# DeltaNet with a routed mixture of experts on one core: ScalarE's spread and table load moved, two products added in the prologue, the constants loaded in three pieces

## The chip, the core and the metric

The kernel runs on one core of one Trainium2 chip. Its metric is the device time of one execution in microseconds (us); three executions were timed, and their median counts. The engines are named TensorE (PE; PEld is its weight load), VectorE (DVE), ScalarE (ACT), GpSimd (POOL) and SyncE (SP, which issues most DMAs).

## The reference, cut to what matters

Per batch and head (4 x 8 of them, 768 steps, 48 columns) a state matrix is read and updated by the delta rule; the outputs of all heads of a token are one row x of 384 values, and each of the 3072 rows goes through the one expert that two softmaxes choose.

```python
k_n = k / (np.linalg.norm(k, axis=-1, keepdims=True) + 1e-06)
for t in range(S):
    y[:, :, t] = einsum('bhd,bhde->bhe', q[:, :, t], state)
    v_old = einsum('bhde,bhd->bhe', state, k_n[:, :, t])
    state = state + beta[t] * outer(k_n[:, :, t], v[:, :, t] - v_old)
x = y.transpose(0, 2, 1, 3).reshape(B * S, H * D)
# g = argmax(x @ w_group); e = argmax(x @ w_expert[g]); weights from two softmaxes
out[n] = g_w[n] * e_w[n] * (relu(x[n] @ w1[g, e]) @ w2[g, e])
```

## The kernel before

The recurrence is cut into 24 chunks of 32 steps (`NCH`, `C`). All four batches stand in the 128 partitions, 32 steps each, and the eight heads lie beside each other. Chunks form groups of four (`RG`). For a group the scores of keys with keys are collected in `gt`, and `inverse(g)` (from L351) turns them over into `m`, scales them, runs a long row of small VectorE products and sums (L428, L434) that solve the triangular system, and at last transposes the result into `mt` (L491). For groups 0 and 1 the norms take a root on ScalarE (L390), later ones do it on GpSimd.

The prologue makes the scores of chunks 0 to 9 in four PSUM homes (`early_gram`, `early_pairs`, L265 to L289) while VectorE inverts group 0. Key and query tiles come by `load_kq`, and a small ScalarE write ahead of each load (`begin`, L881 to L886) sets the time of its issue. `idle(home, n)` (L912) is a product into a PSUM tile that nobody reads: of the identity with the first n columns of the constants from the identity on. It stands twice at the end of the prologue, behind the scores of chunks 8 and 9.

Then the loop `for u in range(NCH + 1)` (L996) goes through the periods; period u advances chunk u (`advance`, L528):
- `begin_a` writes norms times v into PSUM (VectorE, L520, one period ahead); TensorE adds keys times state to it (`a_ps`, L536), ScalarE copies it out (`f`, L542), and TensorE starts `o_ps` (L548);
- `w_ps` (L556) is the inverse times f, read from `mtb`; ScalarE copies it (`w`, L559);
- `s_ps` (L566) adds to the state in PSUM, which ScalarE copies to `s_bd` (L574, two halves; from chunk 19 on one half by ScalarE, L576, and one by VectorE, L578). The next chunk's `a_ps` reads `s_bd`;
- `o_ps` is ended with the masked scores (L585 or L590), copied to `x` (L594), stored, transposed (`t_ps`, L612, `xt`, L618) and multiplied by the router (`l_ps`, L508, `lg`, L625) one period later;
- `gram(u + 10)` makes the scores ten chunks ahead (`g_ps`, L306) until period 13.

`spread(u)` (L336) writes `mtb`, the inverse of a chunk spread to two heads' halves by a factor of 0 or 1 per partition: two ScalarE copies of 128x256, one for each half (VectorE for chunk 0 alone). For the next chunk the front half stands behind `xt`, ahead of `s_bd`, and the back half behind `lg`, in all but the last periods. At the head of a group (u + 1 divisible by 4) both read the `mt` that VectorE has just written.

The order of instructions on each engine is the order in which the program is written, and each engine takes its instructions in that order. The VectorE steps of `inverse` and of the router (`route`) are laid between the steps of a period by `work(n)`, which hands out a budget in fixed portions; this order does not depend on times.

The constants are one array of 853 columns, cut by `cols` into two loads (`load_con`, L203): the first 100 columns at the very start, the other 753 (identity, `before`, `ones`, `desc`, `ids`, `quarter`, `places`, `tie`, `slots`, `expert`) behind the scores of chunk 6 in the prologue. ScalarE loads its function table for square roots at the start and the one for exponentials in period 0, by a dummy activation (L1040).

After the recurrence 16 experts follow (L1225, L1244), two matrix products each, with the gathering and scattering of rows on GpSimd.

Of the kernel before, what the change touches and what calls it, by code (L numbers as in the profile page):

```python
# [26 lines left out]
def constants(n_tokens, seq, n_experts, n_group, n_batch):  # L27

    import numpy as np

    p = np.arange(128)
    i, k = np.meshgrid(np.arange(C), np.arange(C), indexing="ij")
    u = np.arange(n_tokens // 128)

    ids = np.stack([(p[:, None] // C) * seq + p[:, None] % C + u * C - n_tokens,
                    u * 128 + p[:, None] + 1], axis=2)
    out = {
        "upper": np.concatenate([np.where(np.arange(2)[None, :, None] == b % 2, (i < k)[:, None], 0)
                                 .reshape(C, 2 * C) for b in range(n_batch)], axis=0),
        "causal": np.tile(i < k, (n_batch, 1)),  # L40
        "tiny": np.full((128, 1), 1e-36),
        "eps": np.full((128, 1), 1e-6),
        "parity": np.stack([p // C % 2 == b2 for b2 in range(2)], axis=1),
        "ident": (p[:, None] == p[None, :]),
        "before": (p[:, None] < p[None, :]),
        "ones": np.ones((128, 128)),
        "desc": np.tile(np.arange(n_group, 0, -1), (128, RG)),
        "ids": ids.reshape(128, -1),
        "quarter": p[:, None] // 32,

        "places": np.tile(np.arange(2 * TILE), (128, 1)),


        "tie": np.tile(n_experts - 1 - np.arange(n_experts) + (1 << 20) * (np.arange(n_experts) < FIXED), (128, 1)),
        "slots": np.tile(SLOTS, (128, 1)),
        "expert": np.tile(np.arange(n_experts), (128, 1)),
    }
    at, n = {}, 0
    for name, a in out.items():
        at[name] = (n, n + a.shape[1])  # L60
        n += a.shape[1]
    return np.concatenate([a.astype(np.float32) for a in out.values()], axis=1), at
# [3 lines left out]
def deltanet_then_moe(  # L66
# [110 lines left out]
    with ExitStack() as first:  # L177
# [20 lines left out]
        def load_kv(u):  # L198
            nc.sync.dma_start(out=kv_[u % NV], in_=kv_d[u])

        cols = [0, const_at["ident"][0], const_d.shape[1]]

        def load_con(i):  # L203
            part = slice(cols[i], cols[i + 1])
            nc.sync.dma_start(out=con[:, part], in_=const_d[:, part])
# [16 lines left out]
        def of_kv(u):  # L222
            return (kv_[u % NV], [lambda: load_kv(u)])

        def of_block(u):
# [4 lines left out]
            3: [of_kq(RG + 2)],  # L230
            RG: [of_kq(RG + 3), of_kq(0, 1)],
            RG + 1: [of_kq(u, 1) for u in range(1, RG)],
            RG + 2: [of_kv(0), (con[:, cols[1]:], [lambda: load_con(1)])],
            RG + 3: [of_kv(1), of_kq(2 * RG)],
            2 * RG + 1: [of_kq(2 * RG + 1), of_block(LEAD)],
            2 * RG + 3: [of_kq(2 * RG + 2), of_kv(2)],
# [18 lines left out]
        def early_gram(u, home, parts=(0, 1)):  # L255

            kqt = kqt_[u % NB]
            of = slice(parts[0], parts[-1] + 1)
            g_out = home.rearrange("p f (j x) -> p f j x", j=NP)[:, :, :, 0:2 * C].rearrange(
                "p f j (a t) -> p f j a t", a=2)  # L260
            for j in range(NP):
                for b in range(B):
                    for hh in range(2):
                        rows = slice(hh * 64, hh * 64 + D)
                        nc.tensor.matmul(g_out[quads[b], hh, j, of],  # L265
                                         lhsT=kqt[rows, 0, j, quads[b]],
                                         rhs=kqt[rows, of, j, quads[b]], start=True, stop=True,
                                         skip_group_check=True)
            for a in parts:
                nc.scalar.activation(scores(u, a), g_out[:, :, :, a], ACT.Copy)  # L270
# [606 lines left out]
        with tc.manual_schedule(engines={mybir.EngineType.PE, mybir.EngineType.DVE,  # L877
# [33 lines left out]
            nc.gpsimd.tensor_copy(what[:, :, 0:2], cut["ids"].rearrange("p (u c) -> p u c", c=2))  # L911
            def idle(home, n):  # L912

                nc.tensor.matmul(home[:, 0:n], lhsT=ident, rhs=con[:, cols[1]:cols[1] + n], start=True,
                                 stop=True, skip_group_check=True)

            for u in range(2 * RG, LEAD):
                early_gram(u, homes[u % len(homes)])
                begin(after_gram[u])
            idle(homes[2][:, 1], 512)  # L920
# [12 lines left out]
            second = inverse(1)  # L933
            next(second)
            next(second)
            mask(0)
            while leading in behind:
                push(leading)
# [57 lines left out]
            for u in range(NCH + 1):  # L996
# [25 lines left out]
                if u + 1 < NCH:  # L1022
                    mask(u + 1)
                known = u + 1 < NCH and (u + 1) // RG in mts
                if u == NCH - 1:
                    allow(PE_STEP)
                    allow(ACT_STEP)
# [7 lines left out]
                elif u < NCH - 3:  # L1035
                    next(step)
                    next(turned)
                    if u == 0:
                        begin(after_w)
                        nc.scalar.activation(rooted, cut["tiny"], ACT.Exp)  # L1040
                    if known:
                        spread(u + 1, [0])
                    allow(SORT)
                    next(step)
                    if u < NCH - NV:
                        load_kv(u + NV)
                    more_weights(u)
                    work(9)
                    next(step)
# [1 line left out]
                    allow(PE_STEP)  # L1051
                    allow(ACT_STEP)
                    if known:
                        spread(u + 1, [1])
                    for v in ahead_of[u]:
                        gram(v)
                    if ahead_of.get(u + 2):
# [401 lines left out]
```

## Time and profile before

| | us |
|---|---|
| median of 3 runs | 497.13 |
| lowest and highest | 489.25 and 498.51 |
| the profiled execution's own time | 495.36 |
| its span, from the first to the last instruction | 493.6 |
| mean granted TensorE clock in the span | 0.971 |
| busy: TensorE, VectorE, ScalarE, GpSimd | 455.2, 239.0, 191.6, 193.1 |

The profiled execution's time is 1.76 us over its span. A view by stretch gives busy times, a view of waits sums the idle time of an engine before an instruction under what ended it, and a timeline lists instructions in order of time. The busy time of TensorE is modelled and says less than its waits. [...]

### The profile page before, as it was taken

The numbers are of one execution on the slowest core, as the hardware profiler recorded it, in microseconds if no ns is written. First come the engines' busy times: TensorE is split into PE (matmuls) and PEld (weight loads), VectorE is DVE, ScalarE is ACT, GpSimd is POOL, SyncE is SP. The second block draws the span as 40 slices with busy tenths as digits, with TensorE's granted clock in tenths as the row PEclk, the third lists the DMA queues.
The fourth block names the chain that finished last, engine by engine and source line by source line (L and its number), as shares of the span: only waits on it lengthen the run. The fifth ranks groups of instructions, "written<-read, shape, count | busy, mean of one in ns | idle before, by whom it ended". The sixth has DMA issues, their size and how long they took to land.

```text
span 493.6 us, 17165 instructions
## 1 busy us (share of the span) xinstructions
PE 455.2 (92%) x7218; PEld 431.2 (87%) x7218; DVE 239.0 (48%) x834; ACT 191.6 (39%) x421; POOL 193.1 (39%) x322
## 2 busy tenths in 40 slices
PE   3669989999998998989999999999999999999992
PEld 3448878898987987879999999999999999999992
DVE  5999999999999855665211201220211111012210
ACT  3478688877865566551112112111211111111110
POOL 5000303716346213112456356545615653465313
PEclk9999999999996589999999999999999999999998
DMA  5987766776532335125978878957958987788751
GB/s 160 273 208 226 212 176 217 213 201 197 145 126 75 119 112 185 37 64 127 339 241 284 274 208 263 314 166 243 312 173 265 327 280 232 244 303 300 220 199 48
DMA packets 58579, 102.53 MB, mean 208 GB/s; under 512 B 19454, under 2 KB 41913, under 8 KB 58499
## 3 DMA queue, kind: packets, MB, share of 16 engines
q1 hardware_dynamic: 52579, 91.40, 59.4%
q0 software_dynamic: 5920, 10.00, 6.6%
q8 instruction: 58, 0.95, 0.9%
q14 instruction: 22, 0.18, 0.1%
HBM read 87.25 MB, written 14.27 MB: 206 GB/s over the span
## 4 chain that ended last, share of the span: by engine, by line
PE 38%; DVE 20%; issue 13%; POOL 12%; DMA 11%; ACT 4%; SPq 1%; POOLq 0%; DVEq 0%; ACTq 0%
PE h_ps L1225 13%; PE y_ps L1244 12%; POOL xq L1197 6%; DMA out_dram<-yo,to_i 6%; DVE m L434 5%; DVE t_b L428 2%; PE w_ps L556 2%; POOL out_dram L1256 2%; PE s_ps L566 2%; DMA kqt<-in_kq_dram 2%; DVE t_c L428 2%; DVE t_d L428 2%; PE a_ps L536 2%; DMA y_dram<-yq 1%; PE o_ps L548 1%
## 5 line engine op out<-in xcount | busy, mean ns | idle before, releaser
L1244 PE MATMUL y_ps<-hid,w 128*128 128x224 f32 (+15 forms) x768 | 132.2, 331 | 0.0
L1244 PEld LDWEIGHTS y_ps<-hid,w 128*128 128x128 f32 x768 | 129.0, 190 | 0.3
L1225 PE MATMUL h_ps<-xt,w 128*128 128x232 f32 (+14 forms) x720 | 122.8, 330 | 0.7 <-DMA w<-in_w_dram 0.7
L1225 PEld LDWEIGHTS h_ps<-xt,w 128*128 128x128 f32 x720 | 120.1, 190 | 1.3 <-PE y_ps L1244 1.0
L1197 POOL DMA_INDIRECT xq<-x_dram,from_q x92 | 87.7, 954 | 35.1 <-issue 24.4
L1228 ACT ACTIVATE hid<-h_ps 128x448 f32<-128x448 f32 (+15 forms) x64 | 32.1, 501 | 101.9 <-PE h_ps L1225 101.9
L1256 POOL DMA_INDIRECT out_dram<-yo,to_i x32 | 34.0, 1062 | 94.2 <-DVE yo L1294 86.0
L1249 ACT ACTIVATE yt<-y_ps 128x224 f32<-128x224 f32 (+15 forms) x34 | 11.4, 336 | 116.6 <-PE y_ps L1244 114.8
L1247 DVE COPY yt<-y_ps 128x232 f32<-128x232 f32 (+13 forms) x14 | 5.1, 365 | 106.2 <-PE y_ps L1244 106.2
L1294 DVE TENSOR_SCALAR yo<-yr,gate 128x384 f32<-128x384 f32 (+14 forms) x28 | 11.3, 420 | 82.6 <-DMA yr<-y_dram 71.0
L346 ACT ACTIVATE mtb<-mt,con 128x256 f32<-128x256 f32 x46 | 34.3, 751 | 5.8 <-DVE mt L491 5.8
L574 ACT ACTIVATE s_bd<-s_ps 48x768 f32<-48x768 f32 x38 | 30.5, 802 | 4.2 <-PE s_ps L566 2.2
L556 PEld LDWEIGHTS w_ps<-f,mtb 64*64 64x64 f32 x768 | 26.2, 142 | 6.3 <-issue 2.3
L556 PE MATMUL w_ps<-f,mtb 64*64 64x48 f32 x768 | 29.6, 228 | 1.5 <-issue 1.4
L536 PE MATMUL a_ps<-s_bd,kqt 112*32 112x96 f32 x736 | 22.3, 263 | 6.1 <-DVE m L408 2.3
L566 PE MATMUL s_ps<-w,kv 32*112 32x96 f32 x736 | 25.5, 278 | 1.6 <-ACT w L559 0.7
L434 DVE TENSOR_TENSOR m<-m,t_b 128x16 f32<-128x16 f32 (+14 forms) x90 | 26.1, 290 | 0.2
L566 PEld LDWEIGHTS s_ps<-w,kv 32*112 32x112 f32 x736 | 21.6, 183 | 5.0 <-ACT w L559 3.6
L428 DVE TENSOR_TENSOR t_b<-m 128x16 f32<-128x16 f32 (+14 forms) x90 | 25.3, 281 | 0.0
L536 PEld LDWEIGHTS a_ps<-s_bd,kqt 112*32 112x32 f32 x736 | 17.8, 117 | 7.6 <-ACT s_bd L574 5.9
L665 POOL TENSOR_TENSOR acc<-acc,hots 128x16 f32<-128x16 f32 x16 | 7.5, 468 | 40.6 <-DVE hots L663 39.6
L548 PE MATMUL o_ps<-s_bd,kqt 112*32 112x96 f32 x736 | 22.5, 262 | 0.0
(198 smaller groups left out, 631.9 us busy)
## 6 DMA issues: line engine op xcount, KB each, us to landing
w<-in_w_dram SPq DMA_DIRECT2D x29, 1536.0 KB, 9.8
kv<-in_kv_dram SPq DMA_DIRECT2D x24, 416.0 KB, 3.8
kqt<-in_kq_dram SPq DMA_DIRECT2D x20, 448.0 KB, 4.4
kqd<-in_kq_dram SPq DMA_DIRECT2D x28, 192.0 KB, 3.5
x_dram<-x SPq DMA_DIRECT2D x24, 192.0 KB, 3.6
w<-in_w_dram SPq DMA_DIRECT2D x24, 128.0 KB, 4.5
y_dram<-yq SPq DMA_DIRECT2D x36, 84.0 KB, 8.8
yr<-y_dram SPq DMA_DIRECT2D x14, 192.0 KB, 2.5
```

Of the source, the lines that this page charges most:

```text
L346: nc.scalar.activation(to, from_, ACT.Copy, scale=by)
L428: nc.vector.tensor_tensor(tv, left.to_broadcast([128] + like), right.to_broadcast([128] + like), op=ALU.mult)
L434: nc.vector.tensor_tensor(to, to, tv, op=ALU.add)
L536: nc.tensor.matmul(a_ps[quads[b], 2 * j:2 * j + 2, :], lhsT=kqt[0:KR, 0, j, quads[b]], rhs=s_bd[0:KR, b, j], start=False, stop=True, skip_ ...
L556: nc.tensor.matmul(w_ps[b, h], lhsT=mtb[b, h].rearrange("p a i -> p (a i)"), rhs=f[b, h], start=(h == 0), stop=True, skip_group_check=True)
L566: nc.tensor.matmul(s_at[0:KR, b, j], lhsT=k[quads[b], j], rhs=w[quads[b], 2 * j:2 * j + 2], start=(u == 0 and j == 0), stop=True, skip_gro ...
L574: nc.scalar.activation(to, from_, ACT.Copy)
L1197: nc.gpsimd.indirect_dma_start(out=xq[:, g, :], out_offset=None, in_=x_dram[:, :].rearrange("n (q c) -> (n q) c", q=4), in_offset=bass.Ind ...
L1225: nc.tensor.matmul(h_ps[:, k], lhsT=w1[:, j, (f + k) * 128:(f + k + 1) * 128], rhs=xt[:, j, 0:R], start=(j == 0), stop=(j == DC - 1), skip ...
L1228: nc.scalar.activation(hid[:, f:f + 2], h_ps, ACT.Relu)
L1244: nc.tensor.matmul(y_ps, lhsT=w2[:, f, j * 128:(j + 1) * 128], rhs=hid[:, f], start=(f == 0), stop=(f == FC - 1))
L1256: put = nc.gpsimd.indirect_dma_start(out=out[:, :], out_offset=bass.IndirectOffsetOnAxis(ap=to[0:P, i:i + 1], axis=0), in_=yo[0:P, :], in_ ...
```

## The change

- `spread`: where the next chunk is the first of a group, both halves now stand behind `lg`; elsewhere nothing moves.
- The table load for exponentials moves from period 0 to the end of the prologue, behind the root of group 1.
- `idle` now multiplies the identity's first 112 rows with chunk 0's keys, and stands twice more: ahead of the scores of chunk 8, into the third home, and ahead of those of chunk 9, into the fourth.
- The constants are loaded in three pieces: the second (176 columns, identity and `ids`) where the 753 were, the third (577 columns) in period 2.

```diff
@@ constants
         "ident": (p[:, None] == p[None, :]),
+        "ids": ids.reshape(128, -1),
         "before": (p[:, None] < p[None, :]),
         "ones": np.ones((128, 128)),
         "desc": np.tile(np.arange(n_group, 0, -1), (128, RG)),
-        "ids": ids.reshape(128, -1),
@@ loads
-        cols = [0, const_at["ident"][0], const_d.shape[1]]
+        cols = [0, const_at["ident"][0], const_at["before"][0], const_d.shape[1]]
...
-            RG + 2: [of_kv(0), (con[:, cols[1]:], [lambda: load_con(1)])],
+            RG + 2: [of_kv(0), (con[:, cols[1]:cols[2]], [lambda: load_con(1)])],
@@ end of the prologue
             def idle(home, n):
-                nc.tensor.matmul(home[:, 0:n], lhsT=ident, rhs=con[:, cols[1]:cols[1] + n], start=True,
+                keys = kqt_[0][0:KR, 0].rearrange("p j t -> p (j t)")
+                nc.tensor.matmul(home[:, 0:n], lhsT=ident[0:KR], rhs=keys[:, 0:n], start=True,
                                  stop=True, skip_group_check=True)
             for u in range(2 * RG, LEAD):
+                idle(homes[2 + u % 2][:, 0], 512)
                 early_gram(u, homes[u % len(homes)])
...
             next(second)
             next(second)
+            nc.scalar.activation(rooted, cut["tiny"], ACT.Exp)
             mask(0)
@@ period u
+                front = [] if (u + 1) % RG == 0 else [0]
...
                     if u == 0:
                         begin(after_w)
-                        nc.scalar.activation(rooted, cut["tiny"], ACT.Exp)
-                    if known:
-                        spread(u + 1, [0])
+                    if known and front:
+                        spread(u + 1, front)
...
                     if u < NCH - NV:
                         load_kv(u + NV)
+                    if u == 2:
+                        load_con(2)
...
                     if known:
-                        spread(u + 1, [1])
+                        spread(u + 1, range(len(front), 2))
```

On ScalarE, from w of chunk 3 to f of chunk 4, the first head of a group in the loop (`mtb_1354` and `mtb_1399` are the spread of chunk 4). Before:

```order
L559 ACTIVATE w_1346<-w_ps_1329 128x384
L618 ACTIVATE xt_1352<-t_ps_1348 128x384
L346 ACTIVATE mtb_1354<-mt_1277,con 128x8x32
L574 ACTIVATE s_bd<-s_ps 48x16x48 x2
L594 ACTIVATE x_1391<-o_ps_1299 128x384
L625 ACTIVATE lg_996<-l_ps_1393 128x20
L346 ACTIVATE mtb_1354<-mt_1277,con 128x8x32
L542 ACTIVATE f_1435<-a_ps_1325 128x384
```

The same stretch of ScalarE now:

```order
L559 ACTIVATE w_1349<-w_ps_1332 128x384
L618 ACTIVATE xt_1355<-t_ps_1351 128x384
L574 ACTIVATE s_bd<-s_ps 48x16x48 x2
L594 ACTIVATE x_1392<-o_ps_1302 128x384
L625 ACTIVATE lg_998<-l_ps_1394 128x20
L346 ACTIVATE mtb_1399<-mt_1280,con 128x8x32 x2
L542 ACTIVATE f_1438<-a_ps_1328 128x384
```

The front half has gone from ahead of s_bd to ahead of the back half, and both are followed by f; the heads of chunks 8, 12, 16 and 20 read alike.

On TensorE, at the end of the prologue (`home_138` to `home_141` are the four homes; the 32x64 products are the scores of chunks 8 and 9). Before:

```order
L281 MATMUL home_141<-kqt_103 64x64 x16
L265 MATMUL home_138<-kqt_108 32x64 x32
L265 MATMUL home_139<-kqt_109 32x64 x32
L914 MATMUL home_140<-con 128x512
L914 MATMUL a_home<-con 128x384
L556 MATMUL w_ps_792<-f_639,mtb_750 64x48 x16
```

And now:

```order
L281 MATMUL home_141<-kqt_103 64x64 x16
L915 MATMUL home_140<-kqt_100,con 128x512
L265 MATMUL home_138<-kqt_108 32x64 x32
L915 MATMUL home_141<-kqt_100,con 128x512
L265 MATMUL home_139<-kqt_109 32x64 x32
L915 MATMUL home_140<-kqt_100,con 128x512
L915 MATMUL a_home<-kqt_100,con 128x384
L556 MATMUL w_ps_795<-f_639,mtb_752 64x48 x16
```

Two products of 512 columns were added, each ahead of a chunk's scores and into a home that earlier scores must have left.

On ScalarE in the same place (`r` is the root of group 1, `w` that of chunk 0, `rooted` the dummy). Before:

```order
L390 ACTIVATE r_756<-m_753 128x32
L559 ACTIVATE w_809<-w_ps_792 128x384
L884 ACTIVATE wr<-con 128x1
L884 ACTIVATE kqt_100<-con 128x1
L1040 ACT_TABLE_LOAD
L1040 ACTIVATE rooted<-con 128x1
L346 ACTIVATE mtb_816<-mt_748,con 128x8x32
```

And now:

```order
L390 ACTIVATE r_758<-m_755 128x32
L938 ACT_TABLE_LOAD
L938 ACTIVATE rooted<-con 128x1
L559 ACTIVATE w_812<-w_ps_795 128x384
L884 ACTIVATE wr<-con 128x1
L884 ACTIVATE kqt_100<-con 128x1
L346 ACTIVATE mtb_818<-mt_750,con 128x8x32
```

The table load has gone from behind w to ahead of it. VectorE's and GpSimd's instructions stand in the same order in both kernels, row for row; on SyncE one load was added in period 2, behind the values of chunk 5.

## Rows read from the trace of the kernel before

**Rows 1.** Busy time by stretch of the execution: the stretch and its length in us, then for each engine the busy us and, in brackets, the instructions; last the granted TensorE clock as a share of 2.4 GHz, the busy share of the 16 DMA engines and GB/s. The first row is a part of the prologue, the second the periods 0 to 14, the third the periods 15 to 18, the last the experts.
```profile
12.00:30.00 18.00, 10.44 (x447) 8.51 (x430) 17.78 (x88) 10.57 (x37) 0.27 (x1) 1.00 0.83 242
...
36.00:150.00 114.00, 107.76 (x3151) 97.24 (x3147) 111.90 (x435) 87.27 (x174) 40.02 (x116) 1.00 0.66 189
150.00:180.00 30.00, 28.18 (x612) 25.79 (x613) 25.44 (x109) 16.46 (x31) 9.20 (x20) 0.60 0.27 87
...
222.00:493.00 271.00, 261.79 (x1562) 260.31 (x1562) 47.72 (x98) 43.57 (x99) 126.00 (x141) 0.99 0.76 244
```

**Rows 2.** Waits summed (who <- for whom: us in total, times, longest us): the only wait of VectorE over 0.15 us between 12 and 150 us, then one of ScalarE's and two of TensorE's between 36 and 150 us.
```profile
DVE what L774 <- POOL cw L733: 0.7, 1, 0.7
...
ACT mtb L346 <- DVE mt L491: 5.8, 4, 2.3
...
PE a_ps L536 <- ACT s_bd L574: 2.0, 2, 1.2
...
PE a_ps L536 <- DVE a_ps L520: 0.6, 1, 0.6
```

**Rows 3.** ScalarE in order of time at the turn from period 15 to 16 (start us, us, engine, line, operation, out<-in, shape, count, and in brackets the idle time before it and what ended it).
```profile
149.50 0.74 ACT L346 ACTIVATE mtb<-mt,con 128x256 f32<-128x256 f32 x1 [2.20 <-DVE mt L491]
150.14 1.62 ACT L574 ACTIVATE s_bd<-s_ps 48x768 f32<-48x768 f32 x2
...
152.24 0.77 ACT L346 ACTIVATE mtb<-mt,con 128x256 f32<-128x256 f32 x1
153.40 0.49 ACT L542 ACTIVATE f<-a_ps 128x384 f32<-128x384 f32 x1 [0.38 <-PE a_ps L536]
```

**Rows 4.** VectorE at the same turn, in order of time (columns as in rows 3).
```profile
148.17 1.25 DVE L491 STREAM_TRANSPOSE mt<-m 128x1024 f32<-128x1024 f32 x1
...
150.15 0.53 DVE L520 TENSOR_TENSOR a_ps<-kv,normt 128x384 f32<-128x384 f32 x1
```

**Rows 5.** TensorE at the ends of the periods 14 and 15, in order of time (columns as in rows 3).
```profile
141.80 0.84 PE L508 MATMUL l_ps<-wr,xt 128*128 128x20 f32 x6
143.24 0.87 PE L536 MATMUL a_ps<-s_bd,kqt 112*32 112x96 f32 x32 [0.59 <-DVE a_ps L520]
...
146.91 1.04 PE L566 MATMUL s_ps<-w,kv 32*112 32x96 f32 x32
...
148.69 0.85 PE L508 MATMUL l_ps<-wr,xt 128*128 128x20 f32 x6
151.82 1.51 PE L536 MATMUL a_ps<-s_bd,kqt 112*32 112x96 f32 x32 [2.28 <-DVE m L408]
```

**Rows 6.** Busy time by stretch around the time at half clock (columns as in rows 1).
```profile
136.00:151.40 15.40, 12.73 (x428) 11.45 (x418) 15.12 (x48) 9.85 (x20) 8.17 (x27) 1.00 0.43 132
151.40:175.30 23.90, 23.48 (x470) 21.47 (x470) 19.48 (x92) 12.10 (x23) 7.44 (x16) 0.50 0.27 91
```

**Rows 7.** The heads of the groups of chunk 4 and of chunk 12: VectorE's first write of a_ps for chunk 4, and TensorE's first product of the chunks 4 and 12 (columns as in rows 3; no bracket means no idle time over 0.15 us).
```profile
62.19 0.53 DVE L520 TENSOR_TENSOR a_ps<-kv,normt 128x384 f32<-128x384 f32 x1
...
63.87 0.87 PE L536 MATMUL a_ps<-s_bd,kqt 112*32 112x96 f32 x32 [1.21 <-ACT s_bd L574]
...
122.43 0.84 PE L536 MATMUL a_ps<-s_bd,kqt 112*32 112x96 f32 x32
```

**Rows 8.** VectorE in the periods 17 to 19, the last transpose into mt among it, and then ScalarE's f of chunk 20 (columns as in rows 3).
```profile
164.30 0.57 DVE L520 TENSOR_TENSOR a_ps<-kv,normt 128x384 f32<-128x384 f32 x1 [0.97 <-ACT f L542]
...
174.69 0.57 DVE L520 TENSOR_TENSOR a_ps<-kv,normt 128x384 f32<-128x384 f32 x1 [1.92 <-ACT f L542]
...
179.89 1.25 DVE L491 STREAM_TRANSPOSE mt<-m 128x1024 f32<-128x1024 f32 x1
182.23 0.57 DVE L520 TENSOR_TENSOR a_ps<-kv,normt 128x384 f32<-128x384 f32 x1 [1.10 <-ACT f L542]
182.71 0.44 DVE L328 TENSOR_TENSOR gq<-gq,con 128x256 f32<-128x256 f32 x1
185.10 0.96 DVE L578 COPY s_bd<-s_ps 48x768 f32<-48x768 f32 x1 [1.95 <-PE s_ps L566]
...
188.54 0.49 ACT L542 ACTIVATE f<-a_ps 128x384 f32<-128x384 f32 x1
```

**Rows 9.** The end of the prologue on TensorE, then on ScalarE, then on VectorE (columns as in rows 3; L914 are the two products that nothing reads, each of them two matrix instructions).
```profile
30.30 1.18 PE L265 MATMUL home<-kqt 48*32 48x64 f32 x64 [0.63 <-DMA kqt<-in_kq_dram]
31.40 2.07 PE L914 MATMUL home<-con 128*128 128x512 f32 x2
33.62 1.62 PE L914 MATMUL a_home<-con 128*128 128x384 f32 x2
35.17 1.20 PE L556 MATMUL w_ps<-f,mtb 64*64 64x48 f32 x32
...
26.70 3.09 ACT L287 ACTIVATE gq<-home 32x256 f32<-32x256 f32 x8
...
33.73 0.26 ACT L390 ACTIVATE r<-m 128x32 f32<-128x32 f32 x1
...
37.17 1.28 ACT L1040 ACT_TABLE_LOAD   x1
...
35.32 0.17 DVE L392 TENSOR_SCALAR nrm<-r 128x32 f32<-128x32 f32 x1
...
37.38 0.56 DVE L520 TENSOR_TENSOR a_ps<-kv,normt 128x384 f32<-128x384 f32 x1
```


## The prediction

> **What bounds the kernel now.** I read the busy time by stretch first, then the summed waits, then the three engines side by side at one turn of a group of four chunks, last the granted clock. From 36 to 150 us, the state recurrence, TensorE is busy 107.76 of 114.0 us and VectorE 111.90 [rows 1]. Both look full, so the waits must say which one the other waits for: from 12 to 150 us VectorE has no wait over 0.15 us at all (its only listed one comes at 153) [rows 2]. It runs one fixed list of work, the inverses of the groups with the small steps of each period in between, without a hole. ScalarE in the same time waits 5.8 us in four places for mt, which VectorE writes, and TensorE waits 2.0 us for s_bd and 0.6 us for VectorE's a_ps [rows 2]. So VectorE is the spine of this stage, and TensorE and ScalarE catch up with it at the heads of the groups.
>
> At the turn to chunk 16 the reader sees how. VectorE's transpose into mt begins at 148.17 and takes 1.25. ScalarE's first half of the spread waits 2.20 us for it, until 149.50, and s_bd, whose input was ready before, starts behind it at 150.14 and ends at 151.76 [rows 3, 4]. TensorE ends l_ps at 149.54 and starts a_ps of chunk 16 at 151.82, 2.28 us idle [rows 5]. The row names a VectorE line as releaser, but VectorE's a_ps for this chunk was written by 150.68 [rows 4]; the last to come was s_bd at 151.76.
>
> [...] From 222 us on TensorE is 97% busy in the experts (261.79 of 271.0) [rows 1]; no edit touches that stage.
>
> **What the fall of the clock costs.** At half clock VectorE waits for f: 0.97 us before a_ps of chunk 18, 1.92 before that of chunk 19 [rows 8]. Without them its list would be 2.89 us earlier, the last transpose would start at 177.0 instead of 179.89 and end at 178.25. Behind it on VectorE stand a_ps (0.48 to the next start), a mask (0.44) and half of s_bd (0.96) [rows 8]: 180.1. TensorE's a_ps of chunk 20 can start then, and f follows 0.93 later, at 181.0 instead of 188.54 [rows 8]. So the fall costs 7.5 us, and the profiled execution of 495.36 (span 493.6 and 1.76 around it) would have been 487.9. Of the runs shown the fastest took 489.25. I take the middle, 488.6, as the time with an undisturbed clock; the median, 497.13, is 1.77 above the profiled one.
>
> **The change part by part.**
> *The spread at the head of a group.* Five turns (chunks 4, 8, 12, 16, 20). At chunk 16 s_bd could start when s_ps ends, at 146.91 + 1.04 = 147.95 [rows 5], and end 1.62 later at 149.6; what is late next is VectorE's a_ps, 150.68 [rows 4]. TensorE starts near 150.75 instead of 151.82: 1.07 us, and the idle time shrinks from 2.28 to 1.2. Both spread halves (0.74 each [rows 3]) then stand ahead of f and end near 151.7, no later than a_ps does. At chunk 4 it is the same: VectorE's a_ps is there at 62.72, so 63.87 becomes about 62.8, 1.07 us earlier. At chunk 12 TensorE had no idle time, so nothing comes of it [rows 7]. But at chunk 15 TensorE already waits 0.59 us for VectorE [rows 5]: whatever it gained at chunk 4 it stands idle there, 0.59 + 1.07 = 1.66 us. VectorE's order of instructions is the same row for row in both kernels. The stall is moved, then, not taken away: with an undisturbed clock this part is worth 0. At chunk 20 mt comes early enough in the disturbed execution, and both halves behind lg put f back by one half, 0.75 us.
> *The table load.* 1.28 us [rows 9] that stood between w and s_bd of chunk 0 goes into a wait of ScalarE. TensorE's wait for s_bd there is 2.0 - 1.21 = 0.8 us [rows 2, 7]; that much is gained and is given back at chunk 15 like the rest: 0.
> *Two more products in the prologue.* One takes 2.07 us [rows 9]. The first is behind the copies out of its bank: eight take 3.09 from 26.70 on, the fourth ends at 28.24. Upper bound: 28.24 + 2.07, scores of chunk 8 with 1.18, 2.07, scores of chunk 9 with 1.18, 2.07, 1.62 and some 0.05 at each wait give about 38.5 for the first w_ps, which started at 35.17 [rows 9]. VectorE is hit in two places: nrm (35.32) waits for r, which stands on ScalarE behind the copies of chunk 9's scores, and a_ps of chunk 1 (37.38) waits for the last product into its bank: up to 38.4, so 1.0 us later, and that stays until the end. Lower bound: were the products twice as fast because the earlier ones raise the clock, w_ps would start near 35.0 and VectorE would lose nothing; less than nothing isn't to be had, since VectorE has no wait there. I take 0.3, nearer to the lower end, since nrm has 35.32 - 33.99 = 1.3 us of slack [rows 9].
> *The constants.* 577 of 753 columns, 295 KB, leave a stretch in which the DMA engines are 83% busy for one at 66% [rows 1]. What TensorE waits for there now stands behind the first added product, and no reader of those columns comes before period 5: 0, with up to 0.3 us for nothing lost on either side.
>
> [...] The fall came in the longest idle time of TensorE, 2.28 us, and not in 1.21 or 0.59 [rows 5, 7]. [...]
>
> **Does the clock still fall?** The undisturbed schedule has more waits than the trace shows, because VectorE's pace is slower than TensorE's after chunk 14, when the scores ahead end. TensorE needs 143.24 to 149.54, 6.3 us, from a_ps to the end of l_ps [rows 5]. Before chunk 20: a_ps of chunk 19 by VectorE ends at 174.69 - 2.89 + 0.57 = 172.4, TensorE is through at 178.7 and waits until 180.1, 1.4 us. Before chunk 19: a_ps of chunk 18 ends at 164.30 - 0.97 + 0.57 = 163.9, TensorE is through 6.3 us and 0.6 for a group's counts later, at 170.8, and waits until 172.4: 1.6 us (1.1 in the kernel before, which comes there 0.5 later). So instead of 0.59 and 2.28, then 1.1 and 1.4, TensorE meets 1.66, 1.2, 1.6 and 1.4 us: the same idle time in more even pieces, each with only small products around it.
>
> **The sum (forecast).** The clock falls in most executions, at one of these waits. With a fall where it was: 495.36 - 1.07 + 0.75 + 0.3 = 495.3. A fall before chunk 15 leaves more waits in which VectorE's pace lets TensorE catch up (1.2 + 0.4 us more): about 493.7. A fall at chunk 19 leaves less: 497. Likeliest 495, own range 493 to 497.5, chance 0.45.
>
> **Rivals.**
> 1. *The clock stays up*, because no wait is as long as 2.28 us: 488.6 + 0.3 = 489, range 487.5 to 490. For it: 1.21 us at chunk 4 did no harm [rows 7]. Against it: there the wide products of the scores ahead stood beside it; after chunk 14 they don't. Chance 0.32.
> 2. *Slower: the clock falls late*, at the wait before chunk 20. Place: near 179; price: at half clock a period takes 174.69 - 164.30 = 10.4 us [rows 8] against 6.3 to 6.9, and 23.9 us hold 2.3 of them, 8 to 9.4 us, of which nothing is given back since VectorE has no list left that sets the pace. With the upper bound of the prologue, 488.6 + 8.7 + 1.0 = 498.3. It decides if the clock outlasts the three waits before. Chance 0.13.
> 3. *The gains add up*, because VectorE's list isn't the spine, its holes being hidden in its durations: 0.8 + 1.07 + 1.07 from the undisturbed 489.25 gives 486.3. Against it: no wait of VectorE in 138 us [rows 2]. Chance 0.10.
>
> **How the numbers follow.** Forecast 495. The range 487.5 to 499.5 takes in the forecast, rivals 1 and 2 with their bounds, and part of 3. A difference under 2%, about what a measurement of this kernel can tell from none, is 487.2 to 507.1: faster by more is rival 3 alone, 0.10; slower by more would take two falls, 0.03; within, 0.87.
>
> **What would show it.** Right: ScalarE's wait for mt no longer stands before s_bd; a_ps of chunk 16 starts within 0.1 us of VectorE's a_ps; the wait before chunk 15 grows to about 1.7 us, with VectorE as its releaser; mt of chunk 16 at 148 to 149; a stretch at clock 0.50 between 140 and 185. Wrong: the transpose of 148.17 starts 1 us or more earlier; a clock of 1.00 from 36 to 222 (then rival 1); a first w_ps later than 38.5, or two stretches at half clock.

## The result and the profile after

The changed kernel is slower by 0.9%: a median of 495.63 us over 21 runs against 491.98 of the kernel before beside it, ratio 1.0088 (95% interval 1.006 to 1.0116). The lowest times lie 491.97 - 489.22 = 2.75 us apart. The forecast of 495 is close as a number, but it was meant as 2.1 us below the 497.13 of the three runs shown; with 21 runs the kernel before has its median 5.15 us lower, and the sign of the change was missed: that 495 came close is luck. The ratios leave out every run that is slower by more than 1.5% than the fastest of its kernel; the medians take all runs. The profiled execution took 493.46 us, its span 491.6.

Busy time by stretch after the change (columns as in rows 1): the recurrence, the turn of the clock, the experts.

```profile
36.00:150.00 114.00, 110.71 (x3068) 99.35 (x3068) 108.98 (x428) 85.62 (x172) 37.29 (x104) 1.00 0.67 189
150.00:180.00 30.00, 26.58 (x805) 23.71 (x804) 28.87 (x116) 19.65 (x38) 13.46 (x35) 0.89 0.40 123
222.00:491.00 269.00, 259.13 (x1548) 257.31 (x1547) 44.91 (x94) 43.27 (x98) 126.07 (x141) 0.99 0.75 246
```

VectorE, full before with 111.90 us [rows 1], now has 108.98. The fall of the clock costs less than before (0.89 over 150 to 180, where it was 0.60). The experts look alike (TensorE busy 259.13 of 269 us, before 261.79 of 271). So the loss is looked for where VectorE has got holes. Its waits from 12 to 150 us, after:

```profile
DVE a_ps L520 <- ACT f L542: 2.4, 2, 2.0
DVE what L774 <- POOL cw L733: 0.7, 1, 0.7
DVE a_ps L520 <- PE a_home L915: 0.5, 1, 0.5
```

The middle row was there before [rows 2]; the other two are new, 0.52 + 2.04 + 0.41 = 2.97 us of waits before writes of a_ps, where the kernel before had none. In order of time on VectorE (its writes of a_ps for chunks 1, 2 and 5, its transposes for the groups of chunks 4 and 16, and a_ps of chunk 16), then the transpose of chunk 4 in the kernel before:

```profile
38.05 0.57 DVE L520 TENSOR_TENSOR a_ps<-kv,normt 128x384 f32<-128x384 f32 x1 [0.52 <-PE a_home L915]
...
47.97 0.57 DVE L520 TENSOR_TENSOR a_ps<-kv,normt 128x384 f32<-128x384 f32 x1 [2.04 <-ACT f L542]
...
62.97 1.25 DVE L491 STREAM_TRANSPOSE mt<-m 128x1024 f32<-128x1024 f32 x1
...
68.72 0.57 DVE L520 TENSOR_TENSOR a_ps<-kv,normt 128x384 f32<-128x384 f32 x1 [0.41 <-ACT f L542]
...
151.68 1.25 DVE L491 STREAM_TRANSPOSE mt<-m 128x1024 f32<-128x1024 f32 x1
...
153.66 0.53 DVE L520 TENSOR_TENSOR a_ps<-kv,normt 128x384 f32<-128x384 f32 x1
```
```profile
60.16 1.25 DVE L491 STREAM_TRANSPOSE mt<-m 128x1024 f32<-128x1024 f32 x1
```

The transpose of chunk 4 is 2.81 us late, that of chunk 16, with 0.41 more before chunk 5, 3.51 us (148.17 [rows 4]). What f of chunk 1 waited for is on TensorE, from the end of the prologue on; below it stand f itself and, of the kernel before, the second w_ps:

```profile
27.93 2.07 PE L915 MATMUL home<-kqt,con 112*128 112x512 f32 x2 [2.49 <-ACT gq L287]
...
34.17 2.07 PE L915 MATMUL home<-kqt,con 112*128 112x512 f32 x2
36.40 1.62 PE L915 MATMUL a_home<-kqt,con 112*128 112x384 f32 x2
37.94 1.95 PE L556 MATMUL w_ps<-f,mtb 64*64 64x48 f32 x32
40.54 1.82 PE L566 MATMUL s_ps<-w,kv 32*112 32x96 f32 x32 [0.65 <-ACT w L559]
...
45.87 1.51 PE L536 MATMUL a_ps<-s_bd,kqt 112*32 112x96 f32 x32
...
48.08 1.14 PE L556 MATMUL w_ps<-f,mtb 64*64 64x48 f32 x32
```
```profile
47.45 0.49 ACT L542 ACTIVATE f<-a_ps 128x384 f32<-128x384 f32 x1 [1.99 <-PE a_ps L536]
```
```profile
42.43 1.13 PE L556 MATMUL w_ps<-f,mtb 64*64 64x48 f32 x32
```

The reader is to see two delays, one on the other. The first w_ps starts at 37.94 instead of 35.17 [rows 9], behind two more products of 2.07 us. And every product of period 0 takes about 1.7 times as long: w_ps 1.95 against 1.14 at 48.08. That is half clock: a_ps takes 1.51 us at 45.87, as it did at 151.82 [rows 5], where the recorded clock was 0.50 [rows 6]. The first granted clock that this trace records, 1.00, begins at 47.47 (in the trace of before, at 35.35). For the time ahead of its first record the view by stretch prints 1.00 all the same, so neither the 1.00 of 12 to 30 us in rows 1 nor that of 36 to 150 above speaks for the start; the durations do. The records give the clock as a share of full speed; no run shows the frequency named with rows 1. From w_ps to w_ps the period took 10.1 us instead of 7.3.

The part that was thought out in most detail, the spread, did as forecast at this turn. ScalarE at the turn to chunk 16 after the change, to be held against [rows 3], and then TensorE:

```profile
151.54 1.64 ACT L574 ACTIVATE s_bd<-s_ps 48x768 f32<-48x768 f32 x2 [0.77 <-PE s_ps L566]
...
153.66 1.38 ACT L346 ACTIVATE mtb<-mt,con 128x256 f32<-128x256 f32 x2
155.27 0.49 ACT L542 ACTIVATE f<-a_ps 128x384 f32<-128x384 f32 x1 [0.23 <-PE a_ps L536]
```
```profile
146.86 0.87 PE L536 MATMUL a_ps<-s_bd,kqt 112*32 112x96 f32 x32 [0.23 <-ACT s_bd L574]
...
152.16 0.84 PE L508 MATMUL l_ps<-wr,xt 128*128 128x20 f32 x6
154.34 0.87 PE L536 MATMUL a_ps<-s_bd,kqt 112*32 112x96 f32 x32 [1.34 <-DVE a_ps L520]
```

s_bd waits for s_ps alone, both spread halves stand behind it, and TensorE waits for VectorE's a_ps (153.66 + 0.53 = 154.19), 1.34 us where the wait was 2.28 [rows 5]. The clock then fell at 170.35 from 1.00 to 0.50, for 6.8 us.

### The profile page after: what moved, and what is told of

It reads as the page before. It is cut to its first block, busy times and chain, and to the rows that moved or that the text cites. A ratio compares the mean times of both kernels' runs of the same rounds, so it can differ in the third digit from the quotient of the medians.

```text
span 491.6 us, 17168 instructions
## 1 busy us (share of the span) xinstructions
PE 455.5 (93%) x7222; PEld 428.5 (87%) x7222; DVE 238.8 (49%) x834; ACT 191.6 (39%) x421; POOL 193.4 (39%) x322
## 4 chain that ended last, share of the span: by engine, by line
PE 65%; DVE 12%; DMA 9%; POOL 5%; issue 4%; ACT 3%; SPq 1%; POOLq 0%; DVEq 0%; ACTq 0%
PE h_ps L1230 22%; PE y_ps L1249 21%; DMA out_dram<-yo,to_i 5%; PE w_ps L556 4%; DVE m L434 3%; PE s_ps L566 3%; PE l_ps L508 2%; PE a_ps L536 2%; PE o_ps L585 2%; PE g_ps L306 2%; DMA kqt<-in_kq_dram 2%; DMA y_dram<-yq 2%; DVE t_b L428 2%; PE o_ps L548 2%; PE home L915 1%
## 5 line engine op out<-in xcount | busy, mean ns | idle before, releaser
L536 PE MATMUL a_ps<-s_bd,kqt 112*32 112x96 f32 x736 | 20.9, 252 | 3.2 <-DVE a_ps L520 1.3
L434 DVE TENSOR_TENSOR m<-m,t_c 128x28 f32<-128x28 f32 (+6 forms) x84 | 21.5, 255 | 0.0
L380 POOL TENSOR_TENSOR r<-r 128x32 f32<-128x32 f32 x12 | 4.7, 391 | 42.3 <-DVE r L376 41.7
```

Of the source, the lines that this page charges most:

```text
L434: nc.vector.tensor_tensor(to, to, tv, op=ALU.add)
L536: nc.tensor.matmul(a_ps[quads[b], 2 * j:2 * j + 2, :], lhsT=kqt[0:KR, 0, j, quads[b]], rhs=s_bd[0:KR, b, j], start=False, stop=True, skip_ ...
```

## Experiments

Each was run 12 times beside the kernel before (35 runs), four kernels to a chip. The table holds what one profiled execution of each showed: the products that nothing reads in the prologue (count and rows), start of the first w_ps, duration of the first s_ps (1.04 at full clock, 1.82 at half), VectorE's waits before its a_ps of chunks 1, 2 and 5, its transposes for the groups of chunks 4 and 16; then the ratio to the kernel before with its interval; last the median of all runs less that of the kernel before beside it, in us.

| kernel | products | w_ps | s_ps | waits 1, 2, 5 | chunk 4 | chunk 16 | ratio | medians |
|---|---|---|---|---|---|---|---|---|
| before | 2 x 128 | 35.17 | 1.04 | 0, 0, 0 | 60.16 | 148.17 | | |
| changed | 4 x 112 | 37.94 | 1.82 | 0.52, 2.04, 0.41 | 62.97 | 151.68 | 1.0088 (1.006 to 1.0116) | +3.65 |
| e1 | 2 x 112 | 35.51 | 1.82 | 0, 0.61, 1.98 | 60.53 | 150.93 | 1.0039 (0.9998 to 1.008) | +2.28 |
| e2 | 4 x 128 | 35.89 | 1.04 | 0, 0, 0.36 | 60.10 | 149.35 | 0.9997 (0.9941 to 1.0052) | +4.33 |
| e3 | 2 x 112 | 35.69 | 1.82 | 0, 0.79, 0.62 | 60.71 | 149.61 | 1.0009 (0.9977 to 1.0042) | 0.00 |
| e4 | 4 x 128 | 36.41 | 1.04 | 0, 0, 1.83 | 60.39 | 150.24 | 1.0012 (0.9971 to 1.0053) | -0.34 |
| e5 | 4 x 112 | 38.12 | 1.82 | 0.53, 2.02, 0.33 | 63.13 | 151.51 | 1.0047 (1.001 to 1.0085) | +3.12 |
| e6 | 4 x 112 | 38.12 | 1.82 | 0.52, 2.05, 1.51 | 63.16 | 153.85 | 1.0092 (1.005 to 1.0135) | +3.73 |
| e7 | 4 x 112 | 38.27 | 1.82 | 0.52, 1.89, 1.27 | 63.14 | 153.28 | 1.0052 (1.0013 to 1.0091) | +2.80 |
| e8 | 2 x 128 | 35.41 | 1.82 | 0, 0.57, 1.62 | 60.32 | 150.02 | 1.0022 (0.9982 to 1.0061) | +1.80 |
| e9 | 4 x 128 | 36.03 | 1.04 | 0, 0, 0 | 60.02 | 147.97 | 1.0029 (0.9992 to 1.0067) | +1.65 |
| e10 | 2 x 128 | 35.95 | 1.04 | 0, 0, 0 | 60.08 | 148.40 | 0.9958 (0.9926 to 0.9989) | -2.25 |
| e11 | 4 x 128 | 36.86 | 1.04 | 0, 0, 4.68 | 60.81 | 153.70 | 0.9974 (0.9941 to 1.0006) | -1.03 |
| e12 | 2 x 128 | 35.73 | 1.82 | 0, 1.00, 2.21 | 61.23 | 151.52 | 1.0005 (0.9967 to 1.0043) | -0.03 |
| e13 | 2 x 128 | 36.03 | 1.04 | 0, 0, 1.87 | 60.13 | 150.16 | 0.9997 (0.9969 to 1.0026) | -0.18 |
| e14 | 2 x 128 | 36.14 | 1.04 | 0, 0, 1.85 | 60.00 | 150.48 | 0.9975 (0.9942 to 1.0007) | -1.72 |
| e15 | 4 x 112 | 38.37 | 1.82 | 0.50, 1.85, 0.30 | 63.21 | 151.82 | 1.0032 (1.0004 to 1.0061) | +0.70 |
| e16 | 4 x 128 | 36.03 | 1.04 | 0, 0, 0 | 60.50 | 148.86 | 0.9987 (0.9964 to 1.0011) | -1.87 |

**e1 to e4: the count of the products or their operand?**

```diff
e1 (on the changed kernel)
-                idle(homes[2 + u % 2][:, 0], 512)
e2 (on the kernel before)
+                idle(homes[2 + u % 2][:, 0], 512)
e3 (on the kernel before)
-                nc.tensor.matmul(home[:, 0:n], lhsT=ident, rhs=con[:, cols[1]:cols[1] + n], start=True,
+                keys = kqt_[0][0:KR, 0].rearrange("p j t -> p (j t)")
+                nc.tensor.matmul(home[:, 0:n], lhsT=ident[0:KR], rhs=keys[:, 0:n], start=True,
e4 (on the changed kernel): the reverse of e3, and the constants back in one load of the prologue
```

> The changed kernel without the two added products; the two that stood there before still take keys. Theory A (the two products cost by standing ahead of the first w_ps, 2.8 us, and by keeping period 0 at half clock): the first w_ps is back at 35.2 us, the clock is full before 38, the transposes into mt are back near 60.2 and 148.2, and the time is 0.6 to 1.0% below the changed kernel's, 491 to 492. Theory B (the operand does it: products of keys, 112 rows instead of 128, do not raise the clock as those of the constants did): w_ps back at 35.2, but the clock full only past 44, period 0 still about 9 us long, and only 0.2 to 0.3% regained, 494.

> The kernel before with two more products of the constants and nothing else of the change. Theory A: first w_ps near 38, period 0 near 9 us or a little less, the transpose of chunk 4 near 62.5 to 63, time 0.5 to 0.9% above the kernel before. Theory B: the clock is full by 36, the products after that take half as long, first w_ps near 36 to 37 and period 0 about 7, time within 0.3% of the kernel before.

> The kernel before with keys instead of constants in its two products and nothing else of the change. Theory A: same schedule and time as the kernel before, within 0.2%. Theory B: the clock rises only past 44, period 0 takes 9 instead of 7.1 us, time 0.3 to 0.5% above the kernel before.

> The changed kernel with the constants as operand of all four products, and the constants loaded in the prologue as before; the added products, the spread and the table load as changed. Theory A: as the changed kernel, 0.6 to 1.0% above the kernel before. Theory B: clock full by 36, as the kernel before within 0.3%.

Theory A falls in the traces: with two more products of the constants (e2), and with all of the change but the keys and the split constants (e4), period 0 is at full clock and the transpose of chunk 4 stands at 60.10 and 60.39. The times of e4 agree; those of e2 settle nothing, since half of its runs took 495.0 us or more and its median is 494.23 against 489.90. Theory B holds for the clock: with keys the first s_ps took 1.82 in e1 and e3, with four products of constants 1.04 in e2 and e4. But keys in two products alone (e3) are hidden: period 0 takes 10.4 us from w_ps to w_ps, and VectorE waits 0.79. What is in neither theory is that the delay at chunk 4 takes both, the two more products and the late clock. The end of the prologue on TensorE in e2:

```profile
30.91 2.08 PE L914 MATMUL home<-con 128*128 128x512 f32 x2
32.91 0.96 PE L265 MATMUL home<-kqt 48*32 48x64 f32 x64
33.80 1.13 PE L914 MATMUL home<-con 128*128 128x512 f32 x2
35.07 0.88 PE L914 MATMUL a_home<-con 128*128 128x384 f32 x2
35.89 1.13 PE L556 MATMUL w_ps<-f,mtb 64*64 64x48 f32 x32
```

The clock rises within the scores of chunk 9 (its first record is 1.00 from 33.15), the third product takes 1.13 instead of 2.07, and the first w_ps is 0.7 us later than before instead of 2.8.

**e5 to e8: rows or numbers, and the parts by themselves.**

```diff
e5 (on e4)
-                nc.tensor.matmul(home[:, 0:n], lhsT=ident, rhs=con[:, cols[1]:cols[1] + n], start=True,
+                nc.tensor.matmul(home[:, 0:n], lhsT=ident[0:KR], rhs=con[0:KR, cols[1]:cols[1] + n], start=True,
e6: the changed kernel
e7 (on e3): as e2
e8 (on the kernel before): the spread's edit (front, and range(len(front), 2)) alone
```

> As the variant with constants in all four products, but only 112 of their 128 rows multiplied (the identity cut to 112 rows as well), so that the shape is that of the changed kernel's products and the numbers are the constants. If the rows decide when the clock rises, it is full only past 44 us, as in the three kernels with products of keys, and the time is like the changed kernel's, 0.5 to 0.9% above the kernel before. If the keys as numbers decide (or what they are read behind), the clock is full by 33 to 36, first w_ps near 36, and the time that of the kernel before within 0.4%.

> The changed kernel once more, beside the others on one chip. First w_ps near 38, clock full only past 44, period 0 near 9.2 us, VectorE waiting some 2.5 us in its a_ps of chunks 1 and 2; 0.6 to 1.1% above the kernel before.

> The kernel before with four products of keys (the two of before and the two added) and nothing else of the change: spread, table load and constants as before. If late clock and added products together make the loss and nothing else does: clock past 44, first w_ps near 38, period 0 near 9.5 us, transpose of chunk 4 past 62.5, time as the changed kernel's, 0.6 to 1.1% above the kernel before. If the spread, the table or the constants cost something: at most 0.4% above.

> The kernel before with the spread behind lg at the heads of groups, and nothing else. By the prediction: s_bd starts at the end of s_ps at the turns to chunks 4 and 16, a_ps of chunk 16 starts within 0.1 us of the end of VectorE's a_ps, VectorE's transposes do not move by more than 0.3 us, and the time is within 0.3% of the kernel before. By the rival that the gains add up: transposes 1 us earlier per turn, time 0.4% below.

e5 differs from e4 in nothing but 16 rows of four products. The same stretch of TensorE as shown for e2, with the first s_ps, and then the first s_ps of e4:

```profile
31.23 2.08 PE L914 MATMUL home<-con 112*128 112x512 f32 x2
33.23 1.19 PE L265 MATMUL home<-kqt 48*32 48x64 f32 x64
34.35 2.08 PE L914 MATMUL home<-con 112*128 112x512 f32 x2
36.57 1.62 PE L914 MATMUL a_home<-con 112*128 112x384 f32 x2
38.12 1.95 PE L556 MATMUL w_ps<-f,mtb 64*64 64x48 f32 x32
40.72 1.82 PE L566 MATMUL s_ps<-w,kv 32*112 32x96 f32 x32 [0.65 <-ACT w L559]
```
```profile
38.19 1.04 PE L566 MATMUL s_ps<-w,kv 32*112 32x96 f32 x32 [0.65 <-ACT w L559]
```

With 112 rows the first s_ps takes 1.82, as it does with keys, where e4 has 1.04, and VectorE waits 0.53 and 2.02: the two executions differ in the rows, not in the numbers in them. e7 shows the same with nothing else of the change, and is 0.5% slower. e8 did as the prediction said at its turn, a_ps (152.68) 0.15 us behind the end of VectorE's a_ps (152.00 + 0.53), and no gain came of it. Against its expectation its transpose of chunk 16 is 1.85 us late, behind waits of 0.57 and 1.62: with the very prologue of the kernel before, its clock rose late (first record 44.47, in the kernel before 35.35). So the same prologue had the early clock in one execution and the late one in another, and the one profiled execution of the kernel before was an early one.

**e9 to e12: the mend, fillers, the table.**

```diff
e9 (on the changed kernel): idle's product
-                keys = kqt_[0][0:KR, 0].rearrange("p j t -> p (j t)")
-                nc.tensor.matmul(home[:, 0:n], lhsT=ident[0:KR], rhs=keys[:, 0:n], start=True,
+                nc.tensor.matmul(home[:, 0:n].rearrange("p (k c) -> p k c", c=128), lhsT=ident,
+                                 rhs=ident[:, None, :].to_broadcast([128, n // 128, 128]), start=True,
e10 (on the kernel before), at the end of a period's body; e11: the same on e9
+                    if u in range(14, 20):
+                        idle(ps.tile([128, 512], F32, tag="t", name=f"fill{u}"), 512)
e12 (on the kernel before): the dummy Exp from period 0 to behind next(second)
```

> The changed kernel whole, its constants still loaded in period 2, but the four products of the prologue read the identity four times over (all 128 rows) in place of 112 rows of keys. If the rows of the products are what keeps the clock down: full by 33 to 36 us, first w_ps near 36.4, no wait of VectorE over 0.15 us in the a_ps of chunks 1 and 2, transpose of chunk 4 near 60.3, time that of the kernel before within 0.4%, 0.6 to 1% below the changed kernel's. If something else in the change does (the later constants, the table load): clock past 44, first w_ps near 38, time 0.6 to 1.1% above the kernel before.

> The kernel before with one more product of the constants (128 rows, 512 columns, about 1.1 us at full clock) that nothing reads, at the end of each of the periods 14 to 19, where the scores ahead have ended and TensorE waits for VectorE before a_ps. If the falls of the clock after 140 us cost what the prediction reckoned (7.5 us in a disturbed execution): no half-clock stretch between 140 and 215, time 0.5 to 0.9% below the kernel before. If the products only lengthen TensorE's path: up to 6 times 1.1 us, 0.5 to 1.3% above. If the falls are cheap: within 0.3%.

> The changed kernel with the identity in the prologue's products, and the same six products at the ends of the periods 14 to 19. If both parts work: clock full from 33 to 36 on without a fall before 215, time 0.5 to 1% below the kernel before. If the added products only lengthen TensorE's path: 0.5 to 1.3% above.

> The kernel before with the table load moved ahead of period 0 and nothing else. By the prediction: s_bd of chunk 0 0.8 us earlier if the clock is full, TensorE's a_ps of chunk 1 earlier by as much, VectorE's transposes unmoved within 0.3 us, time within 0.3% of the kernel before. By the rival that gains add up: 0.2% below.

e9 keeps the whole change and gives the four products 128 rows: clock up from 32.79, no wait of VectorE before its writes of a_ps, transposes back at 60.02 and 147.97. In the trace that is the delay found and mended. The times say it less sharply: the interval of 1.0029 holds the kernel before, but it also overlaps that of the changed kernel. In e10 no clock below 1.00 stands between 36 and 222 us:

```profile
150.00:180.00 30.00, 29.74 (x866) 23.83 (x856) 28.88 (x118) 22.04 (x43) 12.75 (x27) 1.00 0.47 141
36.00:222.00 186.00, 177.34 (x5002) 156.16 (x5002) 166.98 (x651) 130.22 (x263) 62.62 (x161) 1.00 0.54 157
```

It is 0.4% faster here (but see e13). e11, both together, is level with the kernel before within its interval and 1.1% below the changed kernel's ratio; its profiled execution had another fall, at 54.54 for 10.2 us, and a wait of 4.68 behind it. e12's gain of 0.8 us at the table load went unseen: its clock rose late too, s_bd waited for s_ps instead of the table, and the transposes, expected within 0.3 us, came 1.07 and 3.35 later behind VectorE's waits.

**e13 to e16: on quieter ground.** With the fillers the times scatter less: the highest of the 48 runs is 495.58 us, while 7 of the 35 of the kernel before lie above 496.

```diff
e13: e10 again
e14: e10 and the spread's edit of e8
e15: e10 on e7 (four products of keys)
e16: e10 on e2 (four products of the constants)
```

> The kernel before with the six products at the ends of the periods 14 to 19 once more, as the quiet ground on which the next three differ by one part each. No half-clock stretch between 140 and 215; 0.1 to 0.8% below the kernel before.

> The same with the spread behind lg at the heads of groups. By the prediction (the gain at a head is given back): within 0.15% of the kernel with the six products alone. If the later spread costs something that the falls of the clock have hidden so far: 0.2 to 0.4% above it, with w_ps of chunks 16 and 20 later behind VectorE's a_ps than without.

> The kernel with the six products and four products of keys (112 rows) in the prologue. If the loss is the 2.8 us that VectorE's list falls behind in the a_ps of chunks 1 and 2: transpose of chunk 4 near 63.1, that of chunk 20 near 179, time 2.5 to 3 us above the kernel with the six products alone, and nothing more.

> The kernel with the six products and four products of the constants (128 rows) in the prologue. Clock full by 33 to 36 us, transpose of chunk 4 near 60.1, time within 0.2% of the kernel with the six products alone; a little below it if the early rise spares VectorE its wait of 0.6 to 1.0 us before a_ps of chunk 2 in the executions in which the rise came late.

No cost of the spread shows: e14 lies below e13 (0.9975 against 0.9997, where 0.15% either way was expected), not above. e15 was expected 2.5 to 3 us above the kernel with the fillers alone. Against that one, e13, its median is only 0.88 higher; against e14 and e16, 112 rows against 128, 2.42 and 2.57. In the traces the delay reaches the end of the recurrence: the first product of the experts starts at 218.26 in e15, at 215.78 in e16 and at 216.44 in e13. e13 had an early fall (50.51 to 53.93 us at 0.50), and its VectorE shows how such a fall brings an execution near to e15, whose rows stand second:

```profile
44.88 0.55 DVE L520 TENSOR_TENSOR a_ps<-kv,normt 128x384 f32<-128x384 f32 x1
...
67.35 0.57 DVE L520 TENSOR_TENSOR a_ps<-kv,normt 128x384 f32<-128x384 f32 x1 [1.87 <-ACT f L542]
```
```profile
48.21 0.57 DVE L520 TENSOR_TENSOR a_ps<-kv,normt 128x384 f32<-128x384 f32 x1 [1.85 <-ACT f L542]
...
68.87 0.57 DVE L520 TENSOR_TENSOR a_ps<-kv,normt 128x384 f32<-128x384 f32 x1 [0.30 <-ACT f L542]
```

TensorE's lateness reaches VectorE before chunk 2 or, where it comes later, before chunk 5. In three of the five kernels with four products of 112 rows the second wait is small (0.30 to 0.41) after a first of about 2; in e6 and e7 it is 1.51 and 1.27. But this does not explain the median of e13: e14 had the same early fall (50.35) and the same wait (1.85), and its median is 1.54 us lower. e10's gain of 0.4% did not come again in e13, the same kernel (0.9958 and 0.9997, intervals overlapping): what the fillers give lies between nothing and 0.7%, and no version here is shown twice to beat the kernel before.

The table's columns of waits and transposes hold the account of the whole stage. Add VectorE's waits to the 148.2 of an execution without any, and the transpose of chunk 16 comes out within 1 us in all eighteen executions: 148.2 + 2.97 = 151.2 for the changed kernel (151.68), 148.2 + 3.21 = 151.4 for e12 (151.52), 148.2 + 1.87 = 150.1 for e13 (150.16). In eight of them 0.26 to 1.02 us of waits before chunks 6 and 9 come to those in the table. Over these executions the transpose of chunk 16 stands at 152.4 on average with four products of 112 rows and at 150.0 in the thirteen others, of which two (e11, e12) come as late. So an estimate of what the four products of 112 rows cost there is 2.4 us; the 3.51 above is against an execution of the kernel before in which the clock rose early.

## Why the prediction was wrong

**VectorE as the spine: right.** It is what the account above shows, and what made a small delay last. (The one wait of rows 2 is at 123.83 us, not at 153, where there is another; nothing rests on it.) The same finding that led to "worth 0" for spread and table should have led to the question of what could make VectorE wait.

**The step that failed: the two added products, taken at 0.3 us with an upper bound of 1.0.** The first w_ps at 37.94 is within the bound of 38.5, and VectorE's a_ps of chunk 1 waited 0.52, within the 1.0. But the bound ended there. It took a period 0 at full clock, as rows 9 show it, and set only the length of the products against VectorE. With period 0 at half clock f of chunk 1 comes at 47.45, and the a_ps of chunk 2, which the prediction didn't look at, waits 2.04. Measured: 2.81 us at the transpose of chunk 4, nearly three times the upper bound, where the sum had 0.3 (2.4 by the estimate over all executions). The case of products at twice the speed behind the earlier ones was weighed as the lower bound, and it came in e2, with 128 rows: 1.13 us for the third product behind 2.08 for each of the first two. That the edit also takes 16 rows away stood in the diff (ident[0:KR]) and was costed at nothing.

**The same times, another clock.** In the changed kernel TensorE has no idle time over 0.65 us from 27.93 to the end of a_ps, and is at half clock until 47.47. In e4 and e5 the first two products start within 0.1 us of each other (28.20 and 31.32, 28.11 and 31.23) and take the same time; the clock rises behind them in e4 alone (33.86). By the times of these products the two executions would be alike; the first s_ps took 1.04 us in the one and 1.82 in the other.

**The fall of the clock: right in kind, small in size.** It fell between 140 and 185, at 170.35, but for 6.8 us, not 23.9 [rows 6]. Of the 12 profiled executions without fillers 11 had such a fall, at 151 to 180 us, for 3.4 to 30.7 us. For its own fall of 23.9 us the 7.5 is about right: TensorE's a_ps of chunk 20 starts at 187.61 in the kernel before and at 179.70 in e10, which has no fall (and the fillers), 7.9 apart. But that is a price of the long falls, and the profiled execution of before was a poor base: with 21 runs the median is 491.98, not 495.36. In the kernel before it came in TensorE's longest idle time, 2.28 us [rows 5, 6]; after the change it came right behind a wait of 1.25 us (until 170.19), while the one of 1.34 that ended at 154.34 had no such sequel. So rival 1 rested on too little: one fall in the longest gap does not show that shorter gaps spare the clock.

**The wait before chunk 15: wrong.** It was to grow to 1.66 with VectorE as releaser; it is 0.23, for s_bd. Why is not shown: with period 0 at full clock and the spread moved it is 0.23 in e9 and 1.11 in e4. **Spread at the turns: right** (a_ps of chunk 16 starts 0.15 us behind VectorE's, 0.1 was said). But the sign "mt of chunk 16 at 148 to 149" failed, with 151.68. **Table load, constants: no cost shown** (e12 1.0005; e9 with the split has transposes as early as the kernel before).

**The rivals.** None was the one that came: rival 2 had "the upper bound of the prologue" at 1.0 beside a late fall at 8.7; here the prologue cost 2.8 and the fall lasted 6.8 us. Signs named as wrong, a first w_ps past 38.5 or two stretches at half clock, did not tell it either: the second stretch lies at the start, before the first record.

**What stays open.** The delay of 2.8 us is 0.6% of the time; the changed kernel lost 0.9% twice, and e5 and e7, which have the same delay, 0.5%, with overlapping intervals. No run tells a further cost from scatter; of the candidates e14 speaks against the spread. The constants in three pieces stand in the changed kernel and e6 but not in e5 and e7, and no run tests them alone; e9, which has them, is at 1.0029, e4, which has not, at 1.0012. The experts, which no edit touches, took 270.5 to 275.2 us in the eighteen executions from their first product to the end of the span, so one execution of each can't place the rest. Why the first s_ps came at half clock behind products of 112 rows (1.82 us, seven executions) and at full clock behind four of 128 (1.04, five) is not shown either.

## What to carry to other kernels

An operation that nothing reads is there for its side effect, so cost an edit to it by that: here, behind four filler products with 16 rows fewer, the next period ran at half clock (s_ps 1.82 us, in e4 and e9 with 128 rows 1.04). Where an engine runs a fixed list without a hole, price a delay elsewhere by following it to every place where that engine could come to wait, not only to the first. And take the base from many runs: one profiled execution can be the lucky or the unlucky one.

## What the runs showed of the hardware

Products of 128 x 512 and of 112 x 512 took the same 2.07 to 2.08 us at half clock, but the clock differed after them: with four of 128 rows the first s_ps was at full clock in five of five executions, with two of 128 in four of six, with two or four of 112 in none of seven. The clock also fell soon after an early rise, in e4 (47.51), e11 (54.54), e13 (50.51) and e14 (50.35), where TensorE had just stood idle for 1.02 to 1.49 us among small products; in e9 and e16 it stood idle for 1.01 us in the same place as in e4, and no such fall came. The eleven falls at 151 to 180 us without fillers came in, or up to 2 us behind, waits of 0.92 to 2.76 us. A filler of 512 columns put where TensorE waits took 1.10 us (e10, at 150.80), and the clock stood at 1.00 from 140 to 213 us in all six profiled executions that had it.
